# Gated delta rule and MLP on one core: chunk pairs that begin at chunk 0, and queries loaded four tokens to a row

## The chip, the cores and the metric

The kernel runs on 1 core of a Trainium2 chip. The metric is the device time of one execution in microseconds (us). TensorE is called PE here, VectorE DVE, ScalarE ACT, GpSimd POOL and SyncE SP, as in the profile.

## What is computed

For 4 batches of 8 heads, 768 tokens and 48 channels, a state of 48x48 per head is carried over the tokens, and the outputs go through one MLP:

```python
k_n = k / (np.linalg.norm(k, axis=-1, keepdims=True) + 1e-06)
for t in range(S):
    y[:, :, t] = np.einsum('bhd,bhde->bhe', q[:, :, t], state)
    v_old = np.einsum('bhde,bhd->bhe', state, kt)
    state = state + bt[:, :, :, None] * np.einsum('bhd,bhe->bhde', kt, vt - v_old)
...
h = x @ w_in
g = 0.5 * h * (1.0 + np.tanh(c * (h + 0.044715 * h * h * h)))
return (g @ w_out).astype(np.float32)
```

`x` is `y` with the heads side by side: 3072 rows of 384; `w_in` is 384x2048 and `w_out` 2048x384, all in float32.

## The kernel before

**Chunks.** The 768 tokens are cut into 12 chunks of 64 (`c` = 0 to 11). For each chunk, `prep` loads the keys, norms them (`sq`, `ss`, `sr`, `rn`, `Kn`), and has PE transpose keys and queries into `KQT`; `gram` forms the products of keys with keys (`G`) and of keys with queries (`DT`, masked by `mD`); `inverse` builds the inverse `TT` of a 64x64 triangle from 16x16 blocks by way of `WB`, `DI` and `ET`; `state` uses it: a PE group that the profile calls `ps<-R,TT`, then `U`, the new state `S`, and the output `x` of the chunk. Since `state(c)` needs the state of chunk c-1, the groups `ps<-R,TT` come in the order of the chunks, and they serve as milestones below: "R of chunk 3" is the start of that group of 32 matmuls.

**Pairs.** The 16x16 blocks are inverted in `blocks` by a serial chain of 28 small operations on `Yf` (written `tmp` and `Yf`, lines L808 and L812) between a transpose `Tt` (L793) and the two results `XW` (L817, L821). One such chain handles a pair of chunks (a unit, `UNITS`). Before the change the units are [0], [1, 2], [3, 4], ..., [9, 10], [11]: seven. The chain of unit 0 runs on DVE, all others on POOL. `own(u)` feeds a unit with 64 small matmuls per chunk, and for a unit of one chunk it computes that chunk twice; `back` gives the results back with 128 matmuls a unit.

**Tiles.** `mlp(t)` takes the chunks of a tile: first 16x3 matmuls with `W` (`w_in`; for tile 0 a fourth, with a copy of some rows in `gT`, so that it need not wait for the `x<-x` transfers), then gelu on ACT into `gT`, then 16 matmuls `ps<-W,gT` for each 128 rows of the output. The tiles before are [0], [1, 2], ..., [9, 10], [11]: the first and last have 256 columns, the others 512.

**Order.** Each operation is entered with a cost and a due time (table `O`), and a planner (`Plan.schedule`) sets the order of every engine's queue before the program is built. The queues are in order: an engine that waits holds all that stands behind it. Loads of q, k and v go out on SP's queue; loads of the weights go out on POOL's own queue, between POOL's arithmetic, since they cast float32 to bfloat16. `gate()` lets each load wait for the third load entered before it. Keys, queries and values are read in rows of 48 float32 (192 bytes), two transfers of 192 KB per chunk and tensor. Lines L339, L344, L348, L355 and L363 are helpers (tensor_tensor, copy, activation, matmul, DMA); tell operations on them apart by tile names.

## Time and profile before

| | before |
|---|---|
| median of 3 runs | 295.09 us (293.75 to 295.12) |
| profiled execution, its own time | 293.52 us |
| its span, first to last instruction | 291.8 us |
| PE busy | 242.1 us (83%) |
| DVE, ACT, POOL busy | 158.8, 140.5, 129.2 us |
| moved by DMA | 24.05 MB in 83,450 packets, 77,312 of them under 512 bytes |

The profiled execution stands 1.57 us below the median, and its own time 1.72 us above its span. Busy shares are means over a start in which nothing is ready and a long stretch in which PE hardly stops, so the views below are read by stretches. The digits of PEclk are the clock that PE was granted, in tenths of 2.4 GHz: 5 is 1.2 GHz.

### The profile page before, as it was taken

What the parts mean: (1) busy time and instruction counts of PE and PEld (TensorE: products, weight loads), DVE (VectorE), ACT (ScalarE), POOL (GpSimd) and SP (SyncE); (2) the same over time, 40 slices, a digit from 0 to 9 for tenths busy, and PEclk for the clock granted to TensorE, in tenths of its full rate; (3) what the DMA queues carried; (4) which work ended last, traced back from release to release, by engine and by line L of the source; (5) the groups of instructions that cost most, each with busy time, mean ns of one, the idle gap of its engine ahead of it and who ended that gap; (6) DMA issues with size and microseconds to landing.
All of it is one profiled execution on the core that took longest, in us unless ns stands there. A gap on an engine that the chain in (4) does not pass through costs nothing.

```text
span 291.8 us, 13936 instructions
## 1 busy us (share of the span) xinstructions
PE 242.1 (83%) x6470; PEld 160.3 (55%) x6470; DVE 158.8 (54%) x297; ACT 140.5 (48%) x212; POOL 129.2 (44%) x247
## 2 busy tenths in 40 slices
PE   0724477984969969999799896998999999999994
...
PEclk9965555597588997999799999999999999999999
...
GB/s 118 162 125 122 155 115 100 169 150 132 132 90 40 164 147 108 109 114 99 144 53 6 63 24 97 31 53 42 10 31 56 33 18 2 53 63 2 27 67 68
DMA packets 83450, 24.05 MB, mean 82 GB/s; under 512 B 77312, under 2 KB 82912, under 8 KB 83392
## 3 DMA queue, kind: packets, MB, share of 16 engines
...
q8 instruction: 50, 0.82, 1.2%
...
## 4 chain that ended last, share of the span: by engine, by line
PE 72%; DMA 7%; issue 7%; POOL 6%; SPq 4%; DVE 2%; ACT 1%
PE ps L355 68%; DMA qf<-in_q_dram 5%; SPq L363 4%; PE ps L705 3%; DMA W<-in_moe_w_in_dram 2%; POOL Yf L812 2%; POOL tmp L808 2%; POOL R L941 1%; DVE R L339 1%; POOL W L363 1%; DVE sr L667 1%; POOL XW L817 1%; POOL Yf L803 0%; DVE nw L339 0%; POOL gT L363 0%
## 5 line engine op out<-in xcount | busy, mean ns | idle before, releaser
L348 ACT ACTIVATE gT<-ps 128x512 bf16<-128x512 f32 x96 | 56.6, 599 | 46.0 <-PE ps L355 43.6
L355 PE MATMUL ps<-x,W 128*128 128x512 bf16 (+1 forms) x336 | 76.3, 368 | 0.6 <-DMA W<-in_moe_w_in_dram 0.4
L355 PE MATMUL ps<-W,gT 128*128 128x384 bf16 x384 | 69.6, 334 | 2.6 <-issue 2.6
L355 PEld LDWEIGHTS ps<-W,gT 128*128 128x128 bf16 x384 | 36.3, 99 | 26.6 <-issue 5.0
L355 PEld LDWEIGHTS ps<-x,W 128*128 128x128 bf16 x336 | 31.3, 103 | 26.6 <-ACT gT L348 1.9
L339 DVE TENSOR_TENSOR TT<-ps,DI 128x256 bf16<-128x256 f32 (+4 forms) x39 | 25.1, 647 | 23.7 <-PE ps L355 23.2
L344 DVE COPY osb<-ps 128x384 f32<-128x384 f32 x19 | 10.6, 557 | 49.6 <-PE ps L355 49.5
L803 POOL TENSOR_TENSOR Yf<-Tt,bM 128x512 f32<-128x512 f32 x6 | 7.7, 1280 | 59.4 <-DVE Tt L793 59.4
L348 ACT ACTIVATE KQT<-ps 128x1024 bf16<-128x1024 bf16 (+1 forms) x24 | 23.9, 1006 | 20.4 <-PE ps L705 20.3
L812 POOL TENSOR_TENSOR Yf<-Yf,tmp 128x28 f32<-128x28 f32 (+6 forms) x84 | 29.6, 352 | 6.5
L808 POOL TENSOR_TENSOR tmp<-Yf 128x28 f32<-128x28 f32 (+6 forms) x84 | 28.5, 339 | 6.6
L355 PE MATMUL ps<-KQT 48*32 48x32 bf16 (+1 forms) x1280 | 20.3, 204 | 10.4 <-issue 8.4
L355 PEld LDWEIGHTS ps<-KQT 48*32 48x32 bf16 (+1 forms) x1280 | 15.5, 101 | 14.2 <-issue 10.6
L355 PEld LDWEIGHTS ps<-TT,ET 64*64 64x64 bf16 x768 | 15.4, 115 | 12.3 <-issue 5.9
L355 PE MATMUL ps<-TT,ET 64*64 64x32 bf16 (+1 forms) x768 | 18.1, 181 | 4.5 <-issue 2.5
L339 POOL TENSOR_TENSOR Kn<-kf,rn 128x768 bf16<-128x768 f32 (+1 forms) x12 | 16.9, 1425 | 11.0 <-DVE rn L670 8.9
L348 ACT ACTIVATE G<-ps 128x512 bf16<-128x512 f32 x24 | 13.9, 597 | 14.1 <-PE ps L355 13.8
L348 ACT ACTIVATE U<-ps 128x768 bf16<-128x768 f32 x12 | 9.7, 810 | 21.8 <-PE ps L355 21.6
L743 DVE TENSOR_TENSOR DT<-ps,mD 128x512 bf16<-128x512 f32 x24 | 16.2, 684 | 6.1 <-ACT G L348 5.9
L793 DVE STREAM_TRANSPOSE Tt<-ps 128x1024 f32<-128x1024 f32 x7 | 8.7, 1250 | 17.6 <-PE ps L355 17.5
L348 ACT ACTIVATE x<-ps 128x1024 bf16<-128x1024 f32 x12 | 12.3, 1023 | 8.4 <-PE ps L355 8.1
L339 DVE TENSOR_TENSOR S<-ps,S 128x768 bf16<-128x768 f32 x10 | 9.6, 956 | 11.9 <-PE ps L355 11.9
...
## 6 DMA issues: line engine op xcount, KB each, us to landing
...
```

What stands on the lines that cost most here:

```text
L339: return lambda e: e.tensor_tensor(out() if callable(out) else out, a() if callable(a) else a, b() if callable(b) else b, op)
L344: return lambda e: e.tensor_copy(out, a() if callable(a) else a)
L348: return lambda e: e.activation(out, a() if callable(a) else a, func)
L355: ins = t.matmul(out, lhsT, rhs, start=st, stop=sp_, skip_group_check=skip)
L363: return lambda e: e.dma_start(out, a)
L667: norms(lambda e: e.scalar_tensor_tensor(y_, a_, 1.5, y_, ALU.add, ALU.mult), yn_ + ["nw"], yn_)
L705: ins = e.transpose(tb()[:, m, :], t[:, 2 * m:2 * m + 2, :].rearrange("p h d -> p (h d)"), identB[:, :])
L743: op(d_ps(512), {"dve": lambda e: e.tensor_tensor(pv(DTb[r_][:, ps_, :]), gview(1)(), mD[:, :].unsqueeze(1).unsqueeze(1).to_broadcast([128 ...
L793: op({"dve": 1.4}, {"dve": lambda e: e.transpose(Tt[j][:, 0:1024].rearrange("q (x y) -> q x y", y=32), banks2(h).rearrange("q h (n x) -> q ...
L803: sb_op(512, lambda e: e.tensor_tensor(Yv()[:, :, :, :], tv_, bM[j][:, :, :, :], ALU.mult), [f"Tt{j}", f"bM{j}"], [YN], 0, [(hY, 1)] if u ...
L808: sb_op(2 * s * w, lambda e, s=s, w=w, tv=tv: e.tensor_tensor(tv, Yf[j][:, :, s:s + 1, 0:s].to_broadcast([128, 2, w, s]), Yv()[:, :, s + 1 ...
L812: sb_op(2 * s * w, lambda e, s=s, tv=tv: e.tensor_tensor(Yv()[:, :, s + 1:16, 0:s], Yv()[:, :, s + 1:16, 0:s], tv, ALU.add), [YN, f"tmp{j} ...
```

## The change

The units become [0, 1], [2, 3], ..., [10, 11]: six, none computed twice. The tiles become [0], [1], [2, 3], ..., [10, 11]: again seven, two of them half wide, now the first two. Queries are loaded for two chunks at a time by four transfers of 192 KB, each to 32 partitions in rows of 4 tokens (768 bytes); a new `prepq` casts them in two operations, transposes them with 16 matmuls and evicts them per chunk. Within a chunk the query's tokens then lie in the order (j, t) with token 4t + j, so `mD` is built in that order and the eviction to `x` puts the tokens back, reading PSUM with a step of 16 elements (64 bytes). On the engines: the small mask copies, the addition of 1e-6 and the first `R` go to ACT, the keys of chunk 1 to DVE, and the keys of chunk 3 are normed by ACT's Sqrt like those of chunks 0 to 2 and no more on DVE by iteration. Two dummy activations load ACT's tables early. The weights' loads wait for the first keys or queries only and not for `gate()`. The planner's table is another one, and it counts POOL's loads as a queue of their own.

```diff
-NPE_, GATE = 12, 3
-BURST, SLACK = 1.2, 0.15
-NEAR = dict(pe=0.1, dve=0, act=0, pool=0.5, sp=0.0)
-O = dict(step=37.4, prep=-46.8, prep1=-25.5, gram=-46.1, dt=-16.5, own=-64.9, own1=-11.4, blk=-21.5, 
-         blk1=-49.5, inv=-11.7, st=3.3, x=-1.8, mlpa=-100, m1=2.3, m2=44.0, outs=-100, ldk=-74.9, 
-         ldv=-55.7)
+URGENT = -55.0
+GATE = 3
+XQ_, OQ_ = "sp", "sp"
+BURST, SLACK = 0.6, 0.15
+NEAR = dict(pe=0, dve=0.1, act=0.05, pool=0.3, sp=0.0)
+O = dict(step=35.4, prepq=-61.8, prep=-91.6, prep1=-66.9, gram=-46.7, w2=-60.5, prepq0=-83.5, dt0=-35.9,
+         dt=-18.6, own=-122.9, own0=-66.9, blk0=-55.4, inv0=-99.1, st0=-43.2, own1=-11.9, blk=-40.4,
+         blk1=-35.7, inv=-16.4, st=24.1, x=9.5, mlpa=0, m1=0.8, m2=63.7, outs=300, ldq=-42.8, ldk=-82.1,
+         ldv=-70.4)
...
-    TILES = [[0]] + [[c, c + 1] for c in range(1, NCH - 1, 2)] + [[NCH - 1]]
+    TILES = [[0], [1]] + [[c, c + 1] for c in range(2, NCH, 2)]
...
+        warm = sb("warm", [128, 2], F32)
+        zero("warm0", warm[:, :], 0.1, -99)
+        op({"act": 1.5}, {"act": f_act(warm[:, 0:1], warm[:, 0:1], ACT.Sqrt)}, reads=["warm0"], writes=["warm1"], prio=-99)
...
-            op({"dve": 0.16}, {"dve": f_cp(mD[r, :], mU128[r, r])}, reads=["mU128"], writes=[f"mD{a}"], prio=-45)
...
+            op({"act": 0.26}, {"act": f_act(mD[r, :].rearrange("q (j t) -> q t j", j=4),
+                                       mU128[r, r].rearrange("q (t j) -> q t j", j=4))}, reads=["mU128"], writes=[f"mD{a}"], prio=-45)
...
+        EARLY = {}
+        EARLY.update({(nm, c): [] for nm, n in (("kf", 6), ("vf", 3), ("qf", 3)) for c in range(n)})
+
         def load(nm, c, pr):
-            t, src = {"kf": (kf, k), "qf": (qf, q), "vf": (vf, v)}[nm]
+            after = EARLY[nm, c] if (nm, c) in EARLY else gate()
+            if nm == "qf":
+                for b in range(B):
+                    op({"sp": 0.75}, {"sp": f_dma(
+                        qf[32 * b:32 * b + 32, :, :, :].rearrange("q g j d -> q g (j d)"),
+                        q[b, :, 2 * C * c:2 * C * c + 2 * C, :].rearrange("g (t j) d -> t g (j d)", j=4))},
+                       reads=after, writes=[f"qf_{b}"], prio=pr, dma=f"d_qf{c}", bw=0.65)
+                return
+            t, src = {"kf": (kf, k), "vf": (vf, v)}[nm]
...
-            after = gate()
+            after = ["kf0_0", "kf0_1"]
...
+               reads=["qf_0", "qf_1", "qf_2", "qf_3"],
...
-            return (c + 1) // 2, (c + 1) % 2
-
-        UNITS = [[c for c in (2 * u - 1, 2 * u) if 0 <= c < NCH] for u in range(NU)]
+            return c // 2, c % 2
+
+        UNITS = [[2 * u, 2 * u + 1] for u in range(NU)]
...
-            if c < 3:
+            if c < 4:
                 op({"act": 0.24}, {"act": f_act(sr[j][:, :], ss[j][:, :], ACT.Sqrt)},
                    reads=ssn, writes=[f"sr{j}"], prio=pr)
-                norms(lambda e: e.tensor_scalar(sr[j][:, :], sr[j][:, :], 1e-6, None, op0=ALU.add), [f"sr{j}"], [f"sr{j}"])
+                op({"act": 0.21}, {"act": lambda e: e.activation(sr[j][:, :], sr[j][:, :], ACT.Copy, bias=1e-6)},
+                   reads=[f"sr{j}"], writes=[f"sr{j}"], prio=pr)
...
+        def prepq(t):
+            pr = O['prepq0'] + 5 * t if t < 2 else T(2 * t, O['prepq'])
+            for n in range(2):
+                dst = Qn[:, n, :, :, :, 0:D].rearrange("q a j h d -> q h (a j) d")
+                src = qf[:, 4 * n:4 * n + 4, :, :].rearrange("q (h a) j d -> q h (a j) d", a=2)
+                op({"pool": 0.85, "act": 0.82} if t else {"act": 0.82}, {"pool": f_cp(dst, src), "act": f_act(dst, src)},
+                   reads=[f"qf_{b}" for b in range(B)] + [f"Qz{n}"], writes=[f"Q{n}"], prio=pr + 0.1)
+            h = handle()
+            for n in range(2):
+                def tr(e, n=n):
+                    o = bank(h, n).bitcast(BF16).rearrange("q (c h a j t) -> q a j h c t", c=2, h=4, a=2, j=4)
+                    for a in range(2):
+                        for j in range(4):
+                            ins = e.transpose(o[:, a, j], Qn[:, n, a, j, :, :].rearrange("q h d -> q (h d)"), identB[:, :])
+                    return ins
+                op({"pe": 0.48}, {"pe": tr}, mode="m", bk="l" if t < 2 else "t", nm=8,
+                   reads=[f"Q{n}", "identB"] + [f"qt{t}"] * n, writes=[h + (n,)] + [f"qt{t}"] * (1 - n),
+                   free=[f"T1{c % RB}" for c in (2 * t, 2 * t + 1)], alloc=[(h, 2)] if n == 0 else [],
+                   prio=pr + 0.3)
+            for c in (2 * t, 2 * t + 1):
+                ev = lambda c=c: banks2(h).bitcast(BF16).rearrange("q n (c h x) -> q c n h x", c=2, h=4)[:, c % 2]
+                dst = KQT[c % RB][:, 1, :, :].rearrange("q (h n) x -> q n h x", n=2)
+                op(d_act(1024), {"act": f_act(dst, ev)}, reads=[h + (0,), h + (1,)], writes=[f"T1{c % RB}"], prio=pr + 0.3)
...
-                op({"dve": 0.9 * w} if c == 0 and n == 0 else {"pool": 1.5 * w}, {"pool": f, "dve": f},
+                op({"dve": 0.9 * w} if c == 0 and n == 0 or c == 1 else {"pool": 1.5 * w}, {"pool": f, "dve": f},
...
-            slots = [(c, unit_of(c)[1]) for c in cs] if len(cs) == 2 else [(cs[0], 0), (cs[0], 1)]
+            slots = [(c, unit_of(c)[1]) for c in cs]
...
-                op({"pool": 0.9}, {"pool": lambda e: e.tensor_scalar(R[:, :, :], vf[s][:, :, :], -1.0, None, op0=ALU.mult)}, reads=vn, writes=[f"R{j2}"], prio=pr)
+                op(d_act(NP * D), {"act": lambda e: e.activation(R[:, :, :], vf[s][:, :, :], ACT.Copy, scale=-1.0)}, reads=vn,
+                   writes=[f"R{j2}"], prio=pr)
...
-            op(d_act(1024), {"act": f_act(x4[t % NX][:, :, :, 64 * hf:64 * hf + 64],
-                                          lambda: banks2(ho).rearrange("q h (m b t) -> q (h m) b t", m=2, b=4))},
+            op(d_act(1024), {"act": f_act(x4[t % NX].rearrange("q k b (f t j) -> q f (k b) t j", f=2, j=4)[:, hf],
+                                          lambda: banks2(ho).rearrange("q h (y j t) -> q (h y) t j", y=8, j=4))},
...
+        load("kf", 3, -64)
+        load("vf", 0, -63.5)
+        prepq(0)
         prep(1)
+        load("vf", 1, -63)
+        load("qf", 1, -62)
         W1N = []
         for kt in range(KT):
-            W1N += load_w1(kt, -32 + kt)
-        W4N = load_w4(-29)
-        W1N += load_w1x(-28)
+            W1N += load_w1(kt, -62 + kt)
+        W4N = load_w4(-59)
         prep(2)
-        load("vf", 1, -24)
-        load("kf", 3, -27)
-        load("qf", 3, -26)
-        load("kf", 4, -25)
-        load("qf", 4, -24)
+        prep(3)
+        op({"act": 1.5}, {"act": f_act(warm[:, 1:2], warm[:, 1:2], ACT.Gelu_apprx_tanh)}, reads=["warm0", "sr0", "sr1"],
+           writes=["warm2"], prio=O["prep1"] + 1)
+        prepq(1)
```

The planner writes the queues anew everywhere. The prediction speaks of three places. The first is POOL's queue at the start: the weights' loads (`W`, `gT`) and the head of the first chain on POOL, which begins with `Yf<-Tt,bM`. Before:

```order
L339 TENSOR_TENSOR sq<-kf 128x768
L363 DMA W<-in_moe_w_in_dram 48x2048 x2
L339 TENSOR_TENSOR Kn<-kf,rn 128x16x48
L363 DMA W<-in_moe_w_in_dram 48x2048 x2
L339 TENSOR_TENSOR Kn<-kf,rn 128x16x48
L363 DMA W<-in_moe_w_in_dram 48x2048 x2
L363 DMA gT<-in_moe_w_in_dram 48x2048 x2
L941 TENSOR_SCALAR R<-vf 128x768
L803 TENSOR_TENSOR Yf<-Tt,bM 128x512
```

Now:

```order
L358 TENSOR_TENSOR sq<-kf 128x768
L358 TENSOR_TENSOR Kn<-kf,rn 128x16x48
L382 DMA W<-in_moe_w_in_dram 48x2048 x2
L358 TENSOR_TENSOR Kn<-kf,rn 128x16x48
L382 DMA W<-in_moe_w_in_dram 16x3x2048 x2
L382 DMA W<-in_moe_w_in_dram 48x2048 x4
L382 DMA gT<-in_moe_w_in_dram 48x2048 x2
L358 TENSOR_TENSOR bM<-nbT,mS 128x512
L363 CAST Qn<-qf 128x2x8x48
L382 DMA W<-in_moe_w_out_dram 128x4x384 x4
L848 TENSOR_TENSOR Yf<-Tt,bM 128x512
```

All weights, `w_out` too, are now issued ahead of that chain; before, the last two loads of `w_in` and the four of `w_out` stood behind it.

The second place is DVE's queue from the end of unit 0's chain to the last `TT` of chunk 0, behind which R of chunk 0 stands on PE. Before:

```order
L821 TENSOR_TENSOR XW<-ps,nbT 128x2x16x16
L853 TENSOR_TENSOR WB<-ps,mB 128x384 x2
L853 TENSOR_TENSOR DI<-ps,mB 128x384
L339 TENSOR_TENSOR ET<-ps,mE 128x8x48
L853 TENSOR_TENSOR DI<-ps,mB 128x384
L339 TENSOR_TENSOR ET<-ps,mE 128x8x48
L339 TENSOR_TENSOR TT<-ps,DI 128x8x48 x2
L339 TENSOR_TENSOR TT<-ps,DI 128x8x32
L645 TENSOR_REDUCE ss<-sq 128x16
L339 TENSOR_TENSOR TT<-ps,DI 128x8x32
L339 TENSOR_TENSOR TT<-ps,DI 128x8x16 x2
```

Now (it ends with one `DT` and the last `TT` 128x8x16, which are left off):

```order
L866 TENSOR_TENSOR XW<-ps,nbT 128x2x16x16
L788 TENSOR_TENSOR DT<-ps,mD 128x2x4x64
L898 TENSOR_TENSOR WB<-ps,mB 128x384 x2
L898 TENSOR_TENSOR DI<-ps,mB 128x384 x2
L788 TENSOR_TENSOR DT<-ps,mD 128x2x4x64
L838 STREAM_TRANSPOSE Tt<-ps 128x1024
L358 TENSOR_TENSOR ET<-ps,mE 128x8x48 x2
L898 TENSOR_TENSOR WB<-ps,mB 128x768
L358 TENSOR_TENSOR TT<-ps,DI 128x8x48 x2
L358 TENSOR_TENSOR TT<-ps,DI 128x8x32
L898 TENSOR_TENSOR DI<-ps,mB 128x768
L358 TENSOR_TENSOR TT<-ps,DI 128x8x32
```

`WB` and `DI` of chunk 1 (128x768), three `DT` and the transpose `Tt` of the first POOL chain stand in it; a reduction of keys is gone.

The third place is PE's queue around the first MLP matmuls (`x,W` and `x,gT`, 256 columns each). Before:

```order
L355 MATMUL ps<-R,TT 64x48 x32
L355 MATMUL ps<-identB,XW 32x32 x64
L355 MATMUL ps<-U,Kn 64x48 x32
L355 MATMUL ps<-identB,XW 32x32 x64
L355 MATMUL ps<-DT,U 64x64 x32
L705 MATMUL ps<-identB,Qn 128x128 x8
L355 MATMUL ps<-WB,G 64x48 x32
L355 MATMUL ps<-S,KQT 64x48 x32
L355 MATMUL ps<-x,W 128x256 x3
```

Now:

```order
L374 MATMUL ps<-R,TT 64x48 x32
L374 MATMUL ps<-DI,ET 64x48 x32
L374 MATMUL ps<-U,Kn 64x48 x32
L374 MATMUL ps<-DT,U 64x64 x32
L374 MATMUL ps<-S,KQT 64x48 x32
L374 MATMUL ps<-KQT 64x128 x16
L374 MATMUL ps<-x,W 128x256 x3
```

176 small matmuls stand now from R of chunk 0 to the first MLP matmul, and 296 before. Counted over both listings of PE, with MLP matmuls in columns and all others as "small":

| stretch of PE's queue | before: MLP columns, small | now |
|---|---|---|
| from R of chunk 0 to R of chunk 3 | 40,960 and 1,520 | 37,888 and 1,152 |
| from R of chunk 3 to R of chunk 11 | 162,816 and 3,488 | 150,528 and 3,552 |
| from R of chunk 11 to the end | 95,232 and 64 | 110,592 and 64 |
| ahead of R of chunk 0 | 0 and 659 | 0 and 707 |

The whole program has 299,008 MLP columns before and now, and 5,731 small matmuls before, 5,475 now.

## Rows read from the trace of the kernel before

**Rows 1.** The page: busy tenths of PE and its granted clock in 40 slices.

```profile
PE   0724477984969969999799896998999999999994
...
PEclk9965555597588997999799999999999999999999
```

**Rows 2.** Windows: length, busy PE, PEld, DVE, ACT, POOL, granted clock, DMA share, GB/s.

```profile
45.49:53.72 8.23, 6.82 (x296) 5.95 (x297) 7.92 (x15) 4.71 (x6) 7.21 (x8) 0.50 0.78 99
53.72:60.00 6.28, 6.25 (x119) 4.76 (x120) 4.62 (x8) 2.95 (x4) 2.91 (x2) 0.63 1.15 180
60.00:80.00 20.00, 14.25 (x368) 11.43 (x367) 5.47 (x8) 8.18 (x12) 5.60 (x12) 0.74 0.89 138
80.00:93.00 13.00, 9.74 (x391) 6.72 (x390) 11.22 (x22) 7.23 (x12) 9.63 (x22) 0.87 0.35 61
93.00:113.00 20.00, 17.07 (x472) 10.28 (x470) 11.75 (x18) 10.78 (x18) 8.68 (x10) 0.92 0.92 152
113.00:246.40 133.40, 126.67 (x3858) 79.60 (x3857) 77.14 (x125) 72.81 (x113) 63.42 (x132) 0.99 0.28 55
246.40:288.01 41.61, 41.57 (x313) 25.02 (x312) 5.02 (x10) 15.85 (x26) 0.00 (x0) 1.00 0.14 43
```

**Rows 3.** PE's timeline (start, length): milestones and the longest stall.

```profile
45.49 1.05 PE L355 MATMUL ps<-R,TT 64*64 64x48 bf16 x32 [0.38 <-DVE TT L339]
...
53.72 0.82 PE L355 MATMUL ps<-x,W 128*128 128x256 bf16 x3 [0.44 <-DMA W<-in_moe_w_in_dram]
...
69.52 0.27 PE L355 MATMUL ps<-KQT 48*32 48x32 bf16 x18 [3.94 <-issue]
```

**Rows 4.** DVE's timeline at the start, single operations.

```profile
8.75 0.17 DVE L653 TENSOR_SCALAR sr<-sr 128x16 f32<-128x16 f32 x1 [0.28 <-ACT sr L348]
...
13.43 1.25 DVE L793 STREAM_TRANSPOSE Tt<-ps 128x1024 f32<-128x1024 f32 x1 [1.78 <-PE ps L355]
...
19.17 1.96 DVE L653 TENSOR_SCALAR sr<-sr 128x16 f32<-128x16 f32 x1
...
21.54 0.21 DVE L808 TENSOR_TENSOR tmp<-Yf,ps 128x52 f32<-128x52 f32 x1
...
26.82 0.25 DVE L808 TENSOR_TENSOR tmp<-Yf,ps 128x88 f32<-128x88 f32 x1
...
36.06 0.69 DVE L821 TENSOR_TENSOR XW<-ps,nbT 128x512 bf16<-128x512 f32 x1
```

**Rows 5.** ACT's timeline: a cast of queries, which waits for its load.

```profile
18.02 0.84 ACT L348 ACTIVATE Qn<-qf 128x768 bf16<-128x768 f32 x1 [2.26 <-DMA qf<-in_q_dram]
```

**Rows 6.** POOL's timeline: keys of chunk 1, head of the first chain, a weights' load.

```profile
19.60 1.49 POOL L339 TENSOR_TENSOR Kn<-kf,rn 128x768 bf16<-128x768 f32 x1
...
31.68 1.29 POOL L803 TENSOR_TENSOR Yf<-Tt,bM 128x512 f32<-128x512 f32 x1
...
47.51 1.15 POOL L363 DMA_DIRECT2D W<-in_moe_w_in_dram  x2
```

**Rows 7.** DMA queues, of the first 80 us (queue, packets, MB, share).

```profile
q1 hardware_dynamic: 38240, 7.28, 61.6%
q0 software_dynamic: 2382, 3.27, 29.1%
```

**Rows 8.** The tile XW on DVE: durations min/median/max in ns.

```profile
L817 DVE TENSOR_TENSOR XW<-ps,nbT x1: 691/691/691, 35.3 to 35.3; 128x512 bf16<-128x512 f32 x1
L821 DVE TENSOR_TENSOR XW<-ps,nbT x1: 691/691/691, 36.1 to 36.1; 128x512 bf16<-128x512 f32 x1
```

**Rows 9.** The page: queue of instructions; groups by line (busy, mean ns, idle before).

```profile
q8 instruction: 50, 0.82, 1.2%
...
L743 DVE TENSOR_TENSOR DT<-ps,mD 128x512 bf16<-128x512 f32 x24 | 16.2, 684 | 6.1 <-ACT G L348 5.9
...
L348 ACT ACTIVATE x<-ps 128x1024 bf16<-128x1024 f32 x12 | 12.3, 1023 | 8.4 <-PE ps L355 8.1
L339 DVE TENSOR_TENSOR S<-ps,S 128x768 bf16<-128x768 f32 x10 | 9.6, 956 | 11.9 <-PE ps L355 11.9
```

More of the change, by code (lines that the diff above doesn't have):

```diff
@@ L17 @@
 SLACK = 0.3
+URGENT = -100.0
 BURST = 1.2
@@ L126, in schedule @@
         fetch = Fetch()
-        dma_free = 0.0
+        dma_free = w_free = 0.0
+        queued = []
         bank_free = [0.0] * self.nbanks
@@ L194, in schedule @@
                         pr += 5000.0
-                    far = late > NEAR[e]
+                    far = late > (NEAR[e] if o.prio > URGENT else 0.12)
                     key = (far, t if far else 0.0, pr, i)
@@ L215, in schedule @@
             if o.dma:
-                dma_free = max(o.end + 1.3, dma_free) + o.bw
-                o.lat = dma_free + 0.5 - o.end
+                arrival = o.end + 1.3
+                if e == "pool":
+                    w_free = max(arrival, w_free) + o.bw
+                    o.lat = w_free + 0.5 - o.end
+                    for p in queued:
+                        if p.end + p.lat - 0.5 > arrival:
+                            p.lat += o.bw
+                    if dma_free > arrival:
+                        dma_free += o.bw
+                        dep_cache.clear()
+                    else:
+                        dma_free = w_free
+                else:
+                    dma_free = max(arrival, dma_free) + o.bw
+                    o.lat = dma_free + 0.5 - o.end
+                    queued.append(o)
             free_at[e] = o.end
@@ L432, in bass_deltanet__then__act_gelu_tanh_kernel @@
         bpad = sb("bpad", [128, NP, 2 * NU], F32)
-        bcol = bpad[:, :, 1:NCH + 1]
+        bcol = bpad
         nbT = sb("nbT", [128, NU, 2, 16], F32)
         kf = [sb(f"kf{i}", [128, NP, D], F32) for i in range(RL)]
-        qf = [sb(f"qf{i}", [128, NP, D], F32) for i in range(2)]
+        qf = sb("qf", [128, 8, 4, D], F32)
         vf = [sb(f"vf{i}", [128, NP, D], F32) for i in range(RL)]
@@ L441, in bass_deltanet__then__act_gelu_tanh_kernel @@
         Kn = [sb(f"Kn{i}", [128, NP, 64], BF16) for i in range(RB)]
-        Qn = [sb(f"Qn{i}", [128, NP, 64], BF16) for i in range(2)]
+        Qn = sb("Qn", [128, 2, 2, 4, 2, 64], BF16)
         KQT = [sb(f"KQT{i}", [128, 2, NM, 128], BF16) for i in range(RB)]
@@ L544, in load_w1 @@
         def load_w1(kt, pr):
-            after = gate()
+            after = ["kf0_0", "kf0_1"]
             names = []
@@ L555, in load_w1x @@
         def load_w1x(pr):
-            after = gate()
+            after = ["vf1_0", "vf1_1"]
             names = []
@@ L571, in load_w4 @@
             op({"pool": 0.9}, {"pool": lambda e: e.memset(W4, 0.0)}, writes=W4S, prio=-96)
-            after = gate()
+            after = ["kf0_0", "kf0_1"]
             names = []
@@ L595, in bass_deltanet__then__act_gelu_tanh_kernel @@
             op({"sp": 0.65}, {"sp": f_dma(BL[:, :, dup, :], bfl)}, writes=[f"BL{dup}"], prio=-69, dma="d_BL", bw=0.4)
-        load("qf", 0, -68)
-        load("kf", 1, -67)
-        load("kf", 2, -66)
-        load("qf", 1, -65)
+        load("kf", 1, -68)
+        load("qf", 0, -67)
+        load("kf", 2, -65)
         hb_ = handle()
@@ L711, in prep2 @@
                     dst = KQT[i][:, kk, ms.start:ms.stop, :]
-                    op(d_any(128 * len(ms)) if kk == 0 and c == 0 else d_act(128 * len(ms)), {"act": f_act(dst, ev), "dve": f_cp(dst, ev)}, reads=[h],
+                    op(d_any(128 * len(ms)) if kk == 0 and c < 2 else d_act(128 * len(ms)), {"act": f_act(dst, ev), "dve": f_cp(dst, ev)}, reads=[h],
                        writes=tn[kk] if np_ == 1 else [tn[kk][n]], prio=pr + 0.2 + 0.1 * kk)
```

74 lines of the change are left out of this document (34 added, 40 removed).

## Prediction

> **What bounds the kernel now.** The page's slices come first [rows 1]: PE is busy nearly all the time from the second quarter on, and in the first it is neither busy nor at full clock. So I cut the span at milestones that the program fixes, R of chunk 0, 3 and 11, and read the windows [rows 2]. From R of chunk 11 (246.40) PE does nothing but MLP: 41.61 us for 95,232 columns, which is 0.437 ns a column. From R of chunk 3 to R of chunk 11 it needs 133.40 us for 162,816 columns (71.1 us at that price) and 3,488 small matmuls; the other 62.3 us make 17.9 ns for a small one, its waits included. By these two prices the stretch from R of chunk 0 (45.49) to R of chunk 3 (113.00) would take 40,960 columns = 17.9 us and 1,520 small = 27.1 us, together 45.0. It took 67.5. These 22.5 us, and the 45.5 us before, are where something can be had; behind 113 PE itself is the bound (busy 126.67 of 133.40, then 41.57 of 41.61).
>
> The same rows say where the 22.5 us lie. Until the first MLP matmul (53.72) 296 small ones took 8.23 us instead of 5.3. Then 6.28 us at a clock of 0.63 lose 2.3. From 60 to 80 PE is idle for 5.8 us, 3.94 of them in one stop that no other engine explains ("issue") [rows 3], and the mean clock of 0.74 loses 5.2 more: after that stop the grant fell. From 80 to 93 it is idle for 3.3 us and the clock loses 1.7, from 93 to 113 idle for 2.9 and 1.6. That makes 25.7, some 3 us of it already in the price of the small ones.
>
> What stands ahead of 45.49 is DVE's work on chunk 0, whose last TT releases R [rows 3]. The first MLP matmul came 8.2 us later and was released by a weights' load [rows 3], which POOL had issued only at 47.51, behind its whole first chain that began at 31.68 [rows 6].
>
> **The change, part by part.** *R of chunk 0.* Unit 0 now holds two chunks, so its transpose Tt needs the keys of chunk 1 too. Their Sqrt stands on ACT behind the two query casts, and these need all four query transfers. Before, the load that the cast at 18.02 waited for was the last of 2.16 MB issued till then [rows 5]: 0.12 MB per us. Ahead of the casts now stand 1.77 MB, hence 14.8 us if long rows are no faster; the queue of long weights' rows wrote 3.27 MB in 29.1% of 80 us, in half the bytes that it read, so per byte read it is about twice as fast as the other queue with 7.28 MB in 61.6% [rows 7], and then some 12.5. I take 14.0. Two casts of 0.84 bring 15.7 [rows 5]. From Sqrt's end to Tt's start chunk 0 took 4.7 us (8.75 to 13.43) in half pieces [rows 4]; chunk 1, whole, gets 5.3, and Tt's 1.25 end at 22.2. Two products Yf, a reduction, a reciprocal and two DT (0.684 each [rows 9]) take some 3.6: 25.8. The chain's operations follow each other every 0.29 us (18 steps from 21.54 to 26.82) [rows 4], 28 of them 8.2 us, then XW 1.5: 35.5, against 36.75 before (36.06 and 0.69). From there chunk 0 took 8.74 us to R. Into this DVE now puts three DT, Tt, and WB and DI of chunk 1 (0.956 for the nearest operation of that size [rows 9]): 2.0 + 1.2 + 1.9 = 5.1; out of it goes a reduction of about 0.9, and some 2.5 us in which DVE waited for PE are filled. So 10.4, and R at 45.9. I take 45.5, the old value: what the removed halts give back is paid for the second chunk. Ends: 43.5 with queries at 12.5; 49 if nothing is filled.
>
> One of the halts deserves its rows: the addition of 1e-6 (line L653), now on ACT, took 0.17 us once and 1.96 us another time, until POOL's product Kn (19.60 to 21.09) was over [rows 4, 6]. In the Trainium skill, "SBUF — State Buffer", section "Who interferes with whom", VectorE and GpSimd share a port pair and whoever comes second is blocked for the whole instruction; a `tensor_tensor` with both inputs in SBUF is in it too, which speaks against the move of chunk 1's keys to DVE. By that rule the new Kn on DVE could wait for POOL's 1.5 us square of keys, and the sum would be 1.5 more; the row shows the halt only for the operation that leaves DVE.
>
> *From R to the first MLP matmul.* 176 small matmuls instead of 296, 3.1 us by price, but R, U, DT and the eviction of x follow each other, 5 us with the 1.023 of x [rows 9]: first MLP at 50.5 instead of 53.7, if the weights are there. They are issued ahead of POOL's chain; that chain begins about where it did (31.68 [rows 6]): six more loads, a bM and a cast stand ahead of it, a first R and the halts at gated loads no more.
>
> *From R of chunk 0 to R of chunk 3.* 37,888 columns = 16.6 and 1,152 small = 20.6: 37.2 us. Of the 25.7 us lost before I keep 1.9 up to the first MLP matmul, the 2.3 of the slow clock behind it, half of the 11.0 of 60 to 80 (both half tiles are then at hand, so PE has columns between its small groups, but its instructions still come through a busy DMA) and half of the last 4.5; nothing of 80 to 93, where PE waited for R, U and x of chunks 1 and 2 one after the other, because tile [1, 2] could not start without chunk 2. Sum 12. Ends: 4 (the first two only) and 22.5 (all stays).
>
> *Behind it.* R of chunk 3 to 11: 150,528 columns = 65.8, 3,552 small at 17.9 = 63.6, together 129.4. To the end: 110,592 columns = 48.3 us; that the last tile is whole costs nothing, since PE has columns left from others (41.57 of 41.61 busy at the end before [rows 2]). Removed for good are 256 small matmuls of a seventh unit, which the counts contain. POOL loses a chain of some 16 us (31.68 to 47.51 [rows 6]), off the path: its cover is PE's own work.
>
> *Eviction of x with steps of 64 bytes.* No row shows it on ACT. The nearest is DVE's two XW: L817 reads PSUM in such steps, L821 in order, both 691 ns [rows 8]. So I cost it at nothing; twice the time of each would put 1 us on the first MLP matmul and 12 us on ACT, which is idle half the time. In the Trainium skill, "Advanced Engine Details and Errata", section "Memory Cachelines", a non-contiguous access to PSUM slows significantly (said of matmuls); by it I would add that 1 us, and the row disagrees.
>
> *The sum:* 45.5 + 37.2 + 12 + 129.4 + 48.3 = 272.4, the end of PE. Behind that lay 3.8 us (288.01 to 291.8), and 1.7 us outside the span: 277.9 against the profiled execution's 293.52, which is 1.57 under the median of 295.09. Two terms are rounded upwards (the kept losses, and R at the old value), so I do not add that offset: **278.0**.
>
> **Rivals.** *The stops stay.* If PE's idle time and low clock up to R of chunk 3 cost what they did, 22.5 instead of 12: 288. For it: the clock was 0.5 throughout 45 to 54 and fell again after one stop of 3.94 [rows 2, 3], and the start is as full of small groups as before. Against it: 5.0 of the loss came from chunks 1 and 2 in a row.
>
> *The weights come late.* Ahead of the first MLP matmul 6.1 MB must have landed (20 transfers of q, k, v, beta, ten of `w_in`), and by then 9.6 MB are queued with `w_out` and the next chunks. The first 80 us moved 10.55 MB [rows 7], 0.132 per us: 6.1 MB at 46, in time; but if all is served evenly, at 0.16 (between that and the 180 GB/s of 53.72 to 60 [rows 2]) the last of `w_in` comes at 60, 10 us late: 288.
>
> *Long rows change nothing,* queries land like the load at 18.02: R at 49.5 and 282.
>
> *Slower than before: PE starved of instructions.* 50 transfers brought 13,936 instructions [rows 9], 279 each; up to R of chunk 3 PE now takes some 2,000 matmuls with their weight loads, 14 transfers. Between 20 and 60 us DMA is to carry all weights beside the loads. If each of the 14 stops PE by 1.4 us more than here assumed, the gain is gone. One stop of 3.94 is in the rows, with DMA at 0.89 [rows 2, 3], but the whole of 60 to 80 has only 5.8 us of idle, so 14 such are far off.
>
> **How the numbers follow.** Chances: as forecast (267 to 284) 0.60; stops stay 0.13; weights late 0.13; long rows change nothing 0.05; starved 0.06; the rest, several small losses that end near the old time, 0.03. A measurement tells 0.5%, some 1.5 us, from no change. Faster by more: 0.88, with some of the second and third case allowed to end at the old time; within: 0.04; slower: 0.08. The range goes from 267 (R at 43.5, losses of 4) to 290, the two cases at 288 with their spread.
>
> **What would show it.** R of chunk 0 between 43.5 and 49 and the first MLP matmul about 5 us behind it, released by x and not by a load; R of chunk 3 near 95, R of chunk 11 near 224; no weights' load behind POOL's first chain; PE's mean clock above 0.63 in the ten us after its first MLP matmul. It is wrong if the first MLP matmul waits for `W` beyond 55, if PE's unexplained stops up to R of chunk 3 exceed 10 us, or if the price of a small matmul behind it leaves 16 to 20 ns.

## The result, and the profile after

The changed kernel takes 285.0 us (median of 4 runs, 283.86 to 286.31), the kernel before beside it 294.42 (291.71 to 295.12): ratio 0.970 [0.962, 0.978]. The gain is 9.4 us. It was forecast as 17; direction and range hold, and the question is where the other 7 us went. Executions of one kernel scatter, and each ratio compares the faster executions of both kernels alone, so that it can differ from the quotient of the medians. The profiled execution took 284.78 us, its span 283.0.

The page of the changed kernel, which answers to [rows 1], with its DMA slices and the queue of instructions:

```profile
PE   0574261799969789699889999999999899999995
...
PEclk9999997579998799869999999999999999999999
DMA  7999999990398244901261130041400011002002
...
q8 instruction: 48, 0.79, 1.2%
```

From the seventh to the ninth slice (42 to 64 us) the clock is at 7, 5 and 7, and the DMA engines are full from the second to the ninth. The same milestones as in [rows 2], cut at R of chunk 0, the first MLP matmul, 60, 80, R of chunk 3, R of chunk 11 and the end of PE (same columns; the last row is the ten us behind the first MLP matmul):

```profile
51.95:57.20 5.25, 4.18 (x180) 3.63 (x177) 3.50 (x5) 3.13 (x4) 4.34 (x6) 0.50 0.99 178
57.20:60.00 2.80, 2.80 (x58) 2.02 (x56) 1.33 (x2) 1.19 (x2) 0.00 (x0) 0.50 1.30 196
60.00:80.00 20.00, 18.85 (x604) 15.05 (x594) 14.47 (x28) 12.73 (x18) 5.20 (x4) 0.99 0.39 70
80.00:100.11 20.11, 15.83 (x469) 11.28 (x468) 12.04 (x25) 7.82 (x12) 14.46 (x33) 0.83 0.69 118
100.11:231.62 131.51, 125.04 (x3901) 79.54 (x3900) 79.65 (x119) 71.16 (x110) 57.01 (x109) 0.97 0.27 57
231.62:280.05 48.43, 48.42 (x321) 25.45 (x320) 5.57 (x10) 20.77 (x34) 0.00 (x0) 1.00 0.12 40
57.20:67.20 10.00, 9.32 (x252) 7.22 (x249) 6.22 (x9) 5.12 (x8) 2.29 (x2) 0.85 0.72 112
```

| stretch | before | forecast | after |
|---|---|---|---|
| to R of chunk 0 | 45.49 | 45.5 | 51.95 |
| to R of chunk 3 | 67.51 | 49.2 | 48.16 |
| to R of chunk 11 | 133.40 | 129.4 | 131.51 |
| to PE's end | 41.61 | 48.3 | 48.43 |

Between 60 and 80 PE is now busy for 18.85 of 20 us at a clock of 0.99, where it had 14.25 at 0.74 [rows 2]. One term is far off: R of chunk 0 comes 6.5 us late. PE's timeline there (start, length, in brackets the idle time ahead and what ended it):

```profile
49.68 0.64 PE L374 MATMUL ps<-KQT 48*64 48x128 bf16 x16 [6.08 <-ACT KQT L367]
50.11 1.02 PE L374 MATMUL ps<-TT,ET 64*64 64x16 bf16 x32
51.39 0.64 PE L374 MATMUL ps<-KQT 48*64 48x128 bf16 x16 [0.26 <-ACT TT L906]
51.95 1.05 PE L374 MATMUL ps<-R,TT 64*64 64x48 bf16 x32
```

PE waits 6.08 us for ACT's `KQT`, which chunk 0 does not need: these 16 matmuls are the products of chunk 2, and they stand ahead of the last `TT` of chunk 0. ACT's timeline says what ACT did meanwhile:

```profile
38.02 0.83 ACT L367 ACTIVATE Qn<-qf 128x768 bf16<-128x768 f32 x1
46.82 0.84 ACT L367 ACTIVATE sq<-kf 128x768 f32<-128x768 f32 x1 [7.96 <-DMA kf<-in_k_dram]
47.57 2.06 ACT L367 ACTIVATE KQT<-ps 128x1024 bf16<-128x1024 bf16 x2
```

It stood in its queue behind the square of chunk 4's keys. Their load was issued at 22.42 and landed at 46.8, 24 us later. Meanwhile POOL's queue had sent out the weights:

```profile
24.19 3.17 POOL L382 DMA_DIRECT2D W<-in_moe_w_in_dram  x6
27.35 1.03 POOL L382 DMA_DIRECT2D gT<-in_moe_w_in_dram  x2
...
32.53 3.07 POOL L382 DMA_DIRECT2D W<-in_moe_w_out_dram  x4
39.46 1.27 POOL L848 TENSOR_TENSOR Yf<-Tt,bM 128x512 f32<-128x512 f32 x1 [3.85 <-DVE Tt L838]
```

and this went through the DMA queues in the first 70 us (queue, packets, MB, share; compare [rows 7], of 80 us):

```profile
DMA packets 31788, 10.99 MB, mean 157 GB/s; under 512 B 26176, under 2 KB 31296, under 8 KB 31776
...
q1 hardware_dynamic: 29024, 7.28, 71.5%
q0 software_dynamic: 2752, 3.54, 30.8%
```

These two queues moved 10.82 MB in 70 us, and 10.55 in the first 80 us before. So the first theory, A: R of chunk 0 is late because ACT's queue is in order and the square of chunk 4's keys stands where it does. The rival, B: the early weights fill the DMA engines, and whatever comes through them is late, the keys of chunk 4 and PE's own instructions too; moving the square then uncovers another wait.

### The profile page after: what moved, and what is told of

It is laid out like the page before. It is cut to its first block, busy times and chain, and to the rows that moved or that the text cites. A ratio compares the mean times of both kernels' runs of the same rounds, so it can differ in the third digit from the quotient of the medians.

```text
span 283.0 us, 13380 instructions
## 1 busy us (share of the span) xinstructions
PE 237.0 (84%) x6214; PEld 155.4 (55%) x6214; DVE 151.3 (53%) x274; ACT 138.8 (49%) x221; POOL 115.6 (41%) x217
## 4 chain that ended last, share of the span: by engine, by line
PE 73%; DMA 12%; issue 5%; DVE 4%; ACT 3%; SPq 1%; POOL 0%
PE ps L374 70%; DMA kf<-in_k_dram 10%; DMA vf<-in_v_dram 2%; PE ps L750 2%; PE ps L716 1%; SPq L382 1%; ACT KQT L367 1%; DVE ss L670 1%; DVE sr L693 1%; DVE nw L358 0%; ACT sq L367 0%; DVE TT L358 0%; POOL bM L358 0%; ACT G L367 0%; DVE S L358 0%
## 5 line engine op out<-in xcount | busy, mean ns | idle before, releaser
L374 PEld LDWEIGHTS ps<-x,W 128*128 128x128 bf16 x336 | 29.4, 100 | 26.4 <-ACT gT L367 2.8
L857 POOL TENSOR_TENSOR Yf<-Yf,tmp 128x28 f32<-128x28 f32 (+6 forms) x70 | 24.4, 349 | 5.5
L374 PE MATMUL ps<-KQT 48*32 48x32 bf16 (+1 forms) x1152 | 18.9, 207 | 8.9 <-ACT KQT L367 7.9
L853 POOL TENSOR_TENSOR tmp<-Yf 128x28 f32<-128x28 f32 (+6 forms) x70 | 23.7, 339 | 5.5
L367 ACT ACTIVATE KQT<-ps 128x1024 bf16<-128x1024 bf16 (+1 forms) x23 | 22.6, 1004 | 3.9 <-PE ps L750 3.0
L374 PEld LDWEIGHTS ps<-KQT 48*32 48x32 bf16 (+1 forms) x1152 | 14.3, 102 | 16.3 <-ACT KQT L367 9.1
L358 POOL TENSOR_TENSOR Kn<-kf,rn 128x768 bf16<-128x768 f32 (+1 forms) x11 | 15.8, 1451 | 10.3 <-DVE rn L696 8.2
L374 PE MATMUL ps<-TT,ET 64*64 64x32 bf16 (+1 forms) x768 | 17.5, 181 | 2.8 <-issue 2.8
L367 ACT ACTIVATE x<-ps 128x1024 bf16<-128x1024 f32 x12 | 12.3, 1022 | 13.0 <-PE ps L374 12.9
L848 POOL TENSOR_TENSOR Yf<-Tt,bM 128x512 f32<-128x512 f32 x5 | 6.4, 1283 | 25.8 <-DVE Tt L838 25.8
L358 DVE TENSOR_TENSOR ET<-ps,mE 128x768 bf16<-128x768 f32 (+1 forms) x13 | 11.4, 886 | 10.0 <-PE ps L374 9.9
L367 ACT ACTIVATE U<-ps 128x768 bf16<-128x768 f32 x12 | 9.7, 810 | 13.4 <-PE ps L374 13.2
L358 POOL TENSOR_TENSOR sq<-kf 128x768 f32<-128x768 f32 (+1 forms) x6 | 8.2, 1359 | 19.1 <-DMA kf<-in_k_dram 16.6
```

What stands on the lines that cost most here:

```text
L358: return lambda e: e.tensor_tensor(out() if callable(out) else out, a() if callable(a) else a, b() if callable(b) else b, op)
L367: return lambda e: e.activation(out, a() if callable(a) else a, func)
L374: ins = t.matmul(out, lhsT, rhs, start=st, stop=sp_, skip_group_check=skip)
L848: sb_op(512, lambda e: e.tensor_tensor(Yv()[:, :, :, :], tv_, bM[j][:, :, :, :], ALU.mult), [f"Tt{j}", f"bM{j}"], [YN], 0, [(hY, 1)] if u ...
L853: sb_op(2 * s * w, lambda e, s=s, w=w, tv=tv: e.tensor_tensor(tv, Yf[j][:, :, s:s + 1, 0:s].to_broadcast([128, 2, w, s]), Yv()[:, :, s + 1 ...
L857: sb_op(2 * s * w, lambda e, s=s, tv=tv: e.tensor_tensor(Yv()[:, :, s + 1:16, 0:s], Yv()[:, :, s + 1:16, 0:s], tv, ALU.add), [YN, f"tmp{j} ...
```

## Experiments

The first four ran on one chip beside the kernel before (293.39 us, median of 13 runs), the next four beside 293.04, the last three beside 294.09.

**The square of chunk 4's keys later (theory A).** After planning, `sq` goes behind chunk 0's `x` on ACT and its reduction next to that of chunk 5 on DVE; nothing else moves.

```diff
...
+        for eng, n, behind in (("act", 0, "x0_0"), ("dve", 1, None)):
+            o = P.orders[eng]
+            o.remove(late[4, n].idx)
+            o.insert(o.index(P.last_x0) + 1 if behind else o.index(late[5, 1].idx), late[4, n].idx)
```

> The changed kernel with two instructions moved: the square of chunk 4's keys on ScalarE stands behind the eviction of chunk 0's x, and its sum on VectorE next to that of chunk 5; every other queue as it was. Theory A (chunk 4's keys land at 46.8 us and hold ScalarE's in-order queue, behind it the evictions of the queries of chunks 2 and 3, behind these PE and R of chunk 0): R of chunk 0 at 46 instead of 52, first MLP matmul at 51 instead of 57.2, total 279 to 280. Theory B (something else would be late next, the weights or the second chunk's work on VectorE): R not before 50, total 284 to 285.

Measured: 288.87 us, ratio 0.986 [0.979, 0.993], no better than the changed kernel. ACT no longer waits for those keys, but PE does not get through R of chunk 0 earlier for it:

```profile
32.30 0.29 PE L374 MATMUL ps<-KQT 48*32 48x32 bf16 x25 [4.82 <-issue]
33.52 1.57 PE L374 MATMUL ps<-identB,XW 32*32 32x32 bf16 x103 [0.94 <-DVE XW L864]
38.49 0.53 PE L374 MATMUL ps<-identB,XW 32*32 32x32 bf16 x25 [3.40 <-issue]
...
48.77 0.83 PE L374 MATMUL ps<-R,TT 64*64 64x48 bf16 x23
51.70 0.41 PE L374 MATMUL ps<-R,TT 64*64 64x48 bf16 x9 [2.10 <-issue]
```

"issue" is a stop that no other engine explains. They stand in the middle of a group: ahead of the 350th and the 478th matmul of the trace, and within R, ahead of the 734th (the expectations below say 353rd, 481st and 737th); and the first two lie 128 matmuls apart. The first one ends before DVE has `XW` ready, so PE would have stood there without it. Theory A is not enough.

**w_out waits for the keys of chunk 4.** The four loads of `w_out` keep their place on POOL's queue and get one wait more.

```diff
...
+        for o in w2.values():
+            o.deps |= {keys["kf", 4, a].idx for a in range(2)}
```

> The changed kernel with one more wait: the four loads of w_out wait until the keys of chunk 4 have landed; all queues in the same order. Theory A (the keys are late because the weights fill the DMA engines): keys of chunk 4 land between 37 and 41 us instead of 46.8, R of chunk 0 at 46 to 47, total 279 to 282, the upper end if POOL's chain (39.5 us) is held or w_out then comes late. Theory B (the keys are late for another reason, say their own queue): they land at 45 or later, total 284 to 287.

Measured: 285.40 us, ratio 0.976 [0.969, 0.984], not told apart from the changed kernel. The keys of chunk 4 landed at 42.3, which neither theory said. R of chunk 0 came in two pieces at 49.01 and 51.78; the stops from 26 to 58 us sum to 12.4. The new wait has a price of its own: POOL stood 11.3 us ahead of these loads, and its first chain began at 45.62 instead of 39.46. Holding `w_out` back in this way does not help.

**The old tiles with the new pairs.**

```diff
-    TILES = [[0], [1]] + [[c, c + 1] for c in range(2, NCH, 2)]
+    TILES = [[0]] + [[c, c + 1] for c in range(1, NCH - 1, 2)] + [[NCH - 1]]
```

> The changed kernel with the old MLP tiles ([0], [1,2], ..., [9,10], [11]); pairs, queries and table as changed; the start up to R of chunk 1 has the same queues. If the loss between R of chunk 0 and R of chunk 3 fell because two half tiles are at hand early: 3 to 6 us slower, 288 to 291, lost between R of chunk 1 and R of chunk 3. If it fell because of the pairs and the early weights alone: 284 to 286.

Measured: 295.90 us, ratio 1.018 [1.005, 1.031]: all of the gain is gone, more than either expectation said, and not where it was said, since R of chunk 3 comes at 98.1 (100.11 in the changed kernel). Its windows, from R of chunk 3 to R of chunk 11 and from there on:

```profile
98.10:228.90 130.80, 116.10 (x3772) 77.24 (x3804) 78.89 (x119) 65.70 (x101) 57.31 (x113) 0.91 0.27 52
228.90:292.00 63.10, 60.56 (x436) 33.95 (x440) 7.25 (x13) 24.75 (x42) 0.00 (x0) 1.00 0.13 43
```

R of chunk 11 comes no later (228.9), but less MLP work is done by then: 132,096 columns stand between R of chunk 3 and 11 in PE's queue instead of 150,528, and 138,240 behind it instead of 110,592. These 27,648 more cost 12.1 us at 0.437 ns. From R of chunk 3 to 11 PE is busy for 116.10 us of 130.80, where it was 125.04 of 131.51. My reading, which no run here takes apart: a tile that ends in the first chunk of a pair can only start a pair later, so PE idles while the chunks are worked on and pays at the end. The table of due times stayed the one of the new tiles; what the old tiles would take with a table of their own is not shown.

**The rows of the queries alone.** A program of loads: 3.1 MB of queries in rows of 192 bytes, then in rows of 768, then eight loads of `w_in` (the outputs are zeros).

> Loads alone, one kind after the other, nothing else computed (the output is zeros): 16 transfers of 192 KB of queries in 192-byte rows, then 16 in 768-byte rows, then 8 of w_in with the cast to bfloat16. If a row costs by its count: the first 21 us (148 GB/s), the second 11 to 13 us. If the bytes set the time: both within 10%, near 20 us.

```profile
0.74:19.73 18.99, 0.41 (x1) 1.00 0.95 166
19.73:36.71 16.98, 0.00 (x1) 1.00 0.90 185
```

The phases took 18.99 us (166 GB/s) and 16.98 (185), in one execution. Long rows take 11% less time, so the bytes count far more than the rows.

**No weights (theory B).** The 14 loads of the weights stay where they are, but carry 64 of 2048 and 16 of 384 columns; zeros stand for the rest, written by two operations on ACT and one on POOL.

```diff
...
-                   f_dma(W1[64 * c_:64 * c_ + 48, kt, :], moe_w_in[48 * h0:48 * h0 + 48, :])
+                   f_dma(W1[64 * c_:64 * c_ + 48, kt, 0:64], moe_w_in[48 * h0:48 * h0 + 48, 0:64])
...
-                   f_dma(W2[:, 4 * j:4 * j + 4, :], w2v[:, 4 * j:4 * j + 4, :])
+                   f_dma(W2[:, 4 * j:4 * j + 4, 0:16], w2v[:, 4 * j:4 * j + 4, 0:16])
```

> All 14 loads of the weights keep their place on POOL's queue but carry only the first columns (64 of 2048 of w_in, 16 of 384 of w_out); the rest of W is filled with zeros on chip, so the MLP works on other weights. PE's, DVE's and SP's queues are as in the changed kernel. Theory B (the full DMA engines hold back both the keys of chunk 4 and PE's own instructions): PE's stops without a releaser from 20 to 58 us fall below 2 us in all (12 in the two kernels before), ACT's wait for the keys of chunk 4 (8.0 us) is gone, R of chunk 0 comes at 45 to 46.5 in one piece, first MLP matmul at 50 to 52. Theory A (only the in-order wait on ACT): the wait goes, but the stops at the 353rd and 481st matmul stay at 3 to 5 us and R of chunk 0 comes at 48 to 52.

```profile
30.25 0.29 PE L374 MATMUL ps<-KQT 48*32 48x32 bf16 x25 [2.79 <-issue]
33.44 1.89 PE L374 MATMUL ps<-identB,XW 32*32 32x32 bf16 x128 [2.89 <-DVE XW L864]
...
45.12 0.66 PE L374 MATMUL ps<-R,TT 64*64 64x48 bf16 x23 [0.33 <-DVE TT L358]
46.82 0.41 PE L374 MATMUL ps<-R,TT 64*64 64x48 bf16 x9 [1.04 <-issue]
...
51.24 0.82 PE L374 MATMUL ps<-x,W 128*128 128x256 bf16 x3
```

R of chunk 0 comes at 45.12, released by `TT` on DVE (its last nine matmuls, behind another stop, at 46.82), the first MLP matmul at 51.24, R of chunk 3 at 94.88 and of chunk 11 at 226.16; 279.31 us. ACT does not wait for the keys. The stops from 20 to 58 fell from some 12 to 4.2, not to 2: the one at 30.25 stayed at 2.79 (loads of q, k and v still fill the engines then: their busy share from 20 to 30 is 1.22), but it ends before DVE has `XW` ready. So in this one execution the early weights, by both waits together, cost the start of R of chunk 0 6.8 us, the first MLP matmul 6.0, R of chunk 3 5.2 and the whole 5.5.

**More loads at a quiet time.** Ten further transfers of 192 KB in rows of 192 bytes, issued at 62 us, into rows of the output that are written later.

```diff
...
+            o = op({"sp": 0.75}, {"sp": f_dma(
+                out[b * S + s0:b * S + s0 + 128, :].rearrange("s (h d) -> s h d", d=D),
+                k[b, :, s0:s0 + 128, :].rearrange("h s d -> s h d"))}, dma="d_dump")
```

> Ten more transfers of 192 KB in rows of 192 bytes, issued on SP behind the values of chunk 4 (about 62 us), where the DMA engines were busy for 0.20 of the time; nothing waits for them but the last outputs. Theory B: PE's stops without a releaser from 60 to 80 us grow from 0.4 to 1 us to 3 to 8 us, and they stand 128 matmuls apart; R of chunk 3 comes 3 to 8 us later. Rival (the stops belong to places of the program, not to the DMA engines): the stops in 60 to 80 stay below 1.5 us; R of chunk 3 moves by less than 2 us.

Measured: 284.80 us. From 62 to 80 us the DMA engines are now busy for 0.90 and 0.80 of the time, where it was 0.23 and 0.41:

```profile
62.00:70.00 8.00, 6.91 (x256) 5.61 (x250) 5.50 (x14) 4.60 (x7) 2.29 (x2) 1.00 0.90 154
70.00:80.00 10.00, 9.34 (x184) 7.01 (x185) 6.06 (x11) 5.07 (x8) 2.90 (x2) 0.83 0.80 149
```

PE's stops from 60 to 80 are 2.0 us against 1.0, and R of chunk 3 comes at 101.64 (100.11). That is less than B said; of the rival's two numbers only the second holds. The 1.5 us need no stops: PE now waits 3.42 us for an `x<-x` transfer.

```profile
85.21 1.46 PE L374 MATMUL ps<-x,W 128*128 128x256 bf16 x6 [3.42 <-DMA x<-x]
```

Nor are long stops tied to the casting loads of the weights. In the first profile of the changed kernel they have all landed by 51.1, and yet PE stops 2.54 us at 84.41; the window around it is

```profile
78.00:88.00 10.00, 7.45 (x247) 5.35 (x246) 5.38 (x9) 4.39 (x6) 4.37 (x7) 0.83 0.93 157
...
84.41 0.25 PE L374 MATMUL ps<-WB,G 64*64 64x48 bf16 x2 [2.54 <-issue]
```

In the eight other executions with this order on PE that stop ahead of the 1,626th matmul takes 2.4 to 3.9 us, with the DMA engines busy for 0.92 or more of the eight us ahead of it and only q, k, v and outputs in the queues of data. With more loads it is missing; the engines are busy for 0.50 from 78 to 88 there, but PE's wait of 3.42 us just ahead could hide it too.

**w_out behind the first POOL chain.** The square later as above, and the four loads of `w_out` behind `XW` of the first POOL chain.

```diff
...
+        pool = P.orders["pool"]
+        for j in range(4):
+            pool.remove(w2[j].idx)
+            pool.insert(pool.index(xw[1]) + 1 + j, w2[j].idx)
```

> The square of chunk 4's keys stands later on ACT as in the first experiment, and the four loads of w_out stand on POOL's queue behind the first POOL chain. Theory B: 3.1 MB fewer are read before 55 us, the stops from 36 to 58 fall from some 8 us to 3, R of chunk 0 comes at 46 to 48 in one piece, the first MLP matmul at 51 to 53; the matmuls of w_out start about 70 and may wait for it 0 to 4 us; total 279 to 284. Theory A (ACT's wait alone): no more than the first experiment gave, R of chunk 0 at 48.8 to 52, total 285 to 289.

Measured: 296.09 us, ratio 1.009 [1.003, 1.016], no gain left, which neither theory said. R of chunk 0 came at 50.34 and the first MLP matmul at 54.84; the stops from 36 to 58 sum to 4.8. The gain is lost behind that, as SP's and ACT's timelines show:

```profile
38.76 3.75 SPq L382 DMA_DIRECT2D kf<-in_k_dram  x2
71.19 1.31 SPq L382 DMA_DIRECT2D vf<-in_v_dram  x2
72.68 2.58 SPq L382 DMA_DIRECT2D qf<-in_q_dram  x4
```

```profile
80.57 0.84 ACT L367 ACTIVATE Qn<-qf 128x768 bf16<-128x768 f32 x1 [14.68 <-DMA qf<-in_q_dram]
```

The values of chunk 3 wait by `gate()` for the last load of `w_out`. Issued behind the chain, from 59.5 on, it held all of SP's queue until 71.19 (51.05 in the changed kernel), ACT waited 14.68 us for queries and PE 7.74 for an `x` behind them.

**The weights gated as before.**

```diff
-            after = ["kf0_0", "kf0_1"]
+            after = gate()
...
-               reads=["qf_0", "qf_1", "qf_2", "qf_3"],
+               reads=gate(),
```

> The weights' loads wait as in the kernel before (each for the third load ahead of it), all else as changed, planned anew. If the early weights are what made room for the gain, the first MLP matmul waits for W until 58 to 64 us and the total is 288 to 293, half the gain lost or more. If they cost as much as they bring (theory B), R of chunk 0 comes at 46 to 48, the first MLP matmul at 56 to 58, and the total stays at 283 to 287.

Measured: 296.54 us, ratio 1.023 [1.012, 1.033], slower than either expectation. POOL stands 17.5 us at those loads (waits of POOL: sum, times, longest):

```profile
POOL W L382 <- DMA W<-in_moe_w_in_dram: 12.0, 2, 6.9
...
POOL gT L382 <- DMA W<-in_moe_w_in_dram: 3.0, 1, 3.0
POOL W L382 <- DMA W<-in_moe_w_out_dram: 1.8, 1, 1.8
POOL W L382 <- DMA gT<-in_moe_w_in_dram: 0.7, 1, 0.7
```

Its first chain starts at 49.38 instead of 39.46, the first MLP matmul comes at 64.19 instead of 57.20, without a wait for `W`. R of chunk 0 came at 49.89, and the stops from 20 to 58 still sum to 11.1: the first six loads go out as early as without the gate, and by 52 us 8.35 MB have moved, against 8.93. So this run does not show what R of chunk 0 would be without early weights. It shows that the gate, which makes POOL stand at its loads, costs this order 11.5 us.

**The changed kernel and the moved square, each again.** Unaltered, to see whether the stops come with the program.

> The changed kernel again, unaltered, to see whether its unexplained stops (1.4 us from 20 to 58) and its R of chunk 0 at 51.95 come again. If the stops are a matter of the program (where its instructions stand, what was loaded with them), they come out at 1 to 2 us again and R of chunk 0 at 51 to 53. If they are a matter of the execution, they may be 10 to 12 us, as in the kernels that differ from it only behind these places; R of chunk 0 is then the later of two waits, at 50 to 54. Total 283 to 288 in either case.

> The kernel with the square of chunk 4's keys moved, again unaltered. A matter of the program: stops of 3 to 5 us at the 353rd and 481st matmul and of 2 us at the 737th, R of chunk 0 at 48.8 and 51.7. A matter of the execution: the stops may be 1 to 2 us in all; R of chunk 0 then comes at 45.5 to 47, as without weights.

The changed kernel took 285.0 us again (283.14 to 288.5), ratio 0.975 [0.962, 0.988]. Its profiled execution (288.5 us) shows what the first one did not:

```profile
32.13 0.29 PE L374 MATMUL ps<-KQT 48*32 48x32 bf16 x25 [4.75 <-issue]
...
38.33 0.53 PE L374 MATMUL ps<-identB,XW 32*32 32x32 bf16 x25 [3.33 <-issue]
...
48.61 0.83 PE L374 MATMUL ps<-R,TT 64*64 64x48 bf16 x23
51.82 0.41 PE L374 MATMUL ps<-R,TT 64*64 64x48 bf16 x9 [2.38 <-issue]
```

The stops from 20 to 58 sum to 11.9 us where they had been 1.4, in the same program, and ACT's wait for the keys is 1.45 us where it had been 7.96. The first MLP matmul ends up at the same place (57.33; 57.20 in the first one). The moved square, again (289.05 us), stops for 10.9 us. So the stops belong to the execution, and theory A's experiment had compared two kinds of executions. Of the ten profiled executions of the new pairs with full weights, eight had stops of 10 to 12 us there and two, the first one and the one with more loads, 1.4 and 1.3; these two had the long wait for the keys (7.96 and 6.92). Nor do these stops set the total: the second experiment's execution with 12.4 us of them took 282.32 us, less than the 284.78 of the first one here with 1.4.

**w_out late, without the gate.** As above, with q, k and v not waiting for `w_out`.

```diff
...
+        w2i = {w2[j].idx for j in range(4)}
+        for i in P.orders["sp"]:
+            P.ops[i].deps -= w2i
```

> The w_out kernel above, with its loads of q, k and v no longer waiting for w_out (they waited until 71.2 us there, and PE 7.7 us for an x behind them). Theory B: with the gate gone those loads go out at 48 to 55 again, R of chunk 2 comes at 86 to 90 (100.3 there), total 281 to 286: R of chunk 0 is no earlier than 50, since w_in alone keeps the DMA engines full up to there. Rival: w_out itself is what comes late (it was issued at 59.5 and wanted at 71.9): then PE still waits 3 us or more there and the total is above 288.

Measured: 288.65 us (283.23 to 289.85). R of chunk 0 at 49.52, the first MLP matmul at 56.48, R of chunk 2 at 94.51, no wait of PE for `w_out` or for `x`. The 7.7 us are gone, as B said, and `w_out` did not come too late; but R of chunk 2 and the total missed what B expected. PE's stops were 9.3 us from 58 to 100 in this execution (5.3 in the first one of the changed kernel). With `w_out` out of the way R of chunk 0 is still 4.4 us behind the run without weights, so most of the price is that of `w_in`. No version with the whole weights was measurably faster than the changed kernel.

## Why the prediction was right, and where it was off

*The start of unit 0.* Queries were cast at 13.16 (forecast 14.0), `Tt` ended at 20.26 (22.2), `XW` at 34.18 (35.5). Right, a little better, though not for the reason given: per byte the long rows were not about twice as fast, they took 11% less time, and by that 14.8 us become 13.2. The rival with R of chunk 0 at 49.5 for late queries is out. The keys of chunk 1 took 0.96 us on DVE, but POOL stood idle then (13.42 to 18.11), so the rule on the shared port was not put to the test.

*R of chunk 0, 45.5.* This is the mis-sized term: 51.95, 6.45 us more. The count of DVE's work from `XW` to R was right, as the run without weights shows (45.12; the whole took 279.31 there, with 278.0 forecast). What was missing is the price of the early weights on other transfers. I weighed them only at the first MLP matmul, as "weights come late" (it waited for none), and did not look at what else has to come through the same DMA engines ahead of R: the keys of chunk 4, which ACT's queue put ahead of the queries of chunk 2, and PE's instructions. In the two executions of the changed kernel it was one or the other: 6.08 us for `KQT` in the first, and in the second the stops, behind which the last part of R came at 51.82. The rival "PE starved" had the mechanism, but took its stops to add up. Mostly they do not: the first, 4.8 us, ends while DVE still works at its chain.

*From R to the first MLP matmul:* 5 us forecast, 5.25 measured, not released by a load. Right.

*R of chunk 0 to 3:* 37.2 and 12 kept, 48.16 measured, so 11.0 kept; "the stops stay" (22.5) is out. That this sum fits is partly luck. From 60 to 80, where I kept 5.5 us, 1.4 were lost (1.15 idle, the rest by the clock); from 80 to 100, where I kept 2.3, it was 7.7 (4.28 idle, among it stops of 2.54 and 1.75, and 3.4 by a clock of 0.83). The half tiles explain a part of what was won here: with the old tiles the stretch took 47.4 us for 9,216 columns less (4.0 us by price), so they are worth some 3 us in it. Their greater worth lies behind it, where the old tiles leave 27,648 columns more for the end.

*R of chunk 3 to 11:* a small matmul now costs (131.51 - 65.8) / 3,552 = 18.5 ns against 17.9, so 2.1 us more than forecast; in the other executions with this order on PE the stretch took 129.7 to 134.4, so this is within their scatter. *To the end:* 48.43, 0.13 more. *Behind it:* 3.0 us in the span and 1.7 outside, 0.77 less than the 5.5 of the sum. Together: 6.45 - 1.04 + 2.11 + 0.13 - 0.77 = 6.9, the difference between 277.9 and 284.78.

*The eviction of x* with steps of 64 bytes costs nothing:

```profile
L367 ACT ACTIVATE x<-ps 128x1024 bf16<-128x1024 f32 x12 | 12.3, 1022 | 13.0 <-PE ps L374 12.9
```

1,022 ns against 1,023 [rows 9]. The rule in the Trainium skill, "Advanced Engine Details and Errata", section "Memory Cachelines", which is said of matmuls, does not show on ACT here.

*Other signs:* no weights' load stands behind POOL's first chain; PE's clock in the ten us behind its first MLP matmul is 0.85, above the 0.63 I named. R of chunk 0, 3 and 11 (51.95, 100.11, 231.62) all miss their places by 5 to 8 us; without weights the last two came at 94.88 and 226.16, near 95 and 224. PE's unexplained stops up to R of chunk 3 stayed below the 10 us that I named in the first execution (6.7) and exceeded them in the second (17.3), whose time is only 3.7 us longer: their sum does not tell what they cost.

What stays open: how much of the scatter of this kernel (283 to 288 us) comes from those stops, and why some executions have them and some not; and how much of the gain is due to the pairs, the queries, the moves between engines and the new table each, since only the tiles and the gate were taken back alone.
